# Linear attention and a Fourier mix: key pieces, masks and conversions of the first batch in other places of a fixed order, folded sums on one engine, and the last group's pieces paced otherwise

## Chip, cores and metric

The kernel runs on one core of a Trainium2 chip. The metric is the device time of one execution in microseconds, as the median of several runs. A profiled execution gives a trace besides: what each engine did and when. The engines are PE (TensorE: matmuls and transposes), DVE (VectorE), ACT (ScalarE), POOL (GpSimd) and SP, which here only issues transfers.

## The reference

Two parts follow each other. The first is a "delta rule" linear attention for B = 4 batches, H = 8 heads, S = 768 tokens, D = 48. Every head carries a 48x48 state through the tokens, one after the other:

```python
k_n = k / (np.linalg.norm(k, axis=-1, keepdims=True) + 1e-06)
for t in range(S):
    y[:, :, t] = np.einsum('bhd,bhde->bhe', q[:, :, t], state)
    v_old = np.einsum('bhde,bhd->bhe', state, kt)
    state = state + bt[:, :, :, None] * np.einsum('bhd,bhe->bhde', kt, vt - v_old)
```

The heads are then laid side by side (768 tokens x 384 channels per batch), and the second part is a Fourier mix with an MLP:

```python
mixed = np.real(np.fft.fft(np.fft.fft(x, axis=1), axis=2))
u = x + mixed
un = (u - mean(u)) / np.sqrt(var(u) + 1e-06)
return u + np.maximum(un @ w_ch1, 0.0) @ w_ch2
```

w_ch1 is 384x1536 and w_ch2 1536x384; both come as float64 and all else is float32.

## The kernel before

**Attention.** Tokens are cut into chunks of 64, so a batch has 12 chunks and the whole work 48 chain steps m. A step (`chain`, L671-728) has three parts: pc products of keys and state, with U = V − pc on DVE; products with the inverted triangular matrix wt, copied by ACT; and the state's sum `st` on DVE. Each part waits for the one before, so the chain is a string of short hand-overs between PE, DVE and ACT. After every second step two chunks' outputs `y` are computed (`outputs`, L732-769: products py, then an ACT copy and a DVE sum into x).

Four chunks form a quad Q, two quads a group g (eight steps). What a group's steps need is made ahead in *pieces*: `prepare` (L413-484; `keys` and `queries` are halves of it) transposes keys and queries (pt on PE, KQT on ACT), makes their grams (pg on PE, A on ACT), and for the queries a masked gram LQ. In the first quads the mask is a multiply of its own on DVE, `masks(Q)` (L405-411, two instructions a quad). `invert(g)` (L500-572) inverts the triangular matrices by 30 pairs of DVE operations (A, then X), and `Merge`/`merge` (L574-648) joins blocks to larger ones (pj on PE, wt on ACT). `values` and `loads` issue the transfers of v, k and q on SP, most of them at L219.

**Fourier and MLP.** `fourier(b)` (L798-920) starts when a batch's outputs are complete. `folded` (L816-828) adds and subtracts the token halves (into scr, or hT for batch 0), then folds the channels: the sum F<-scr at L826 and a small copy of two edge columns at L828. `shifted` (L830-841) builds six combinations of the three tiles. Then come matmuls pf, ACT copies to F, matmuls pb, DVE sums into x, and the layernorm's statistics. `mlps` (L924-991) is one generator over all batches: normalise (un), transpose (ptr, unT), 12 blocks of ph with a ReLU on ACT, and po products that DVE adds to x; then the store.

**Weights.** A float64 weight is turned into float32 in three moves (L300-315): `digits`, two ACT operations; `joined`, two DVE operations and one add on POOL. The first weight is twelve pieces (`FirstWeight`, L317-356): `fetch` starts the transfer, `split(p)` runs the digits, `join` yields after each of its 36 operations, and fetches pieces 10 and 11 on SP into the stages of pieces 0 and 1. `second_weight` (L358-386) does the same with three stages that lie in x tiles of later batches.

**What sets the order.** Through the first batch the order on PE, DVE and ACT is written out by hand (`strict`, L123-137; it holds each instruction behind the one before in the program; POOL and DMA are free). The loop at L1086-1122 goes over steps m = 1 to 11 and, after each of the three parts i, emits other work: `key_work` (L1083) gives how many of the twelve key pieces of quads 4 and 5 (eight pt with their copies, four pg) come after part i of step m; `rest` (L1084) is a sequence of the 36 join operations and the 2 masks of quad 3; `masks(1)`, `masks(2)`, `w.split(10)` and `w.split(11)` have fixed steps; at steps 10 and 11 the first `fourier(0)` begins. From step 12 on (L1131-1212) a scheduler orders the instructions by their dependencies and by the order of emission, and the loop paces that emission: each part of a step adds to `due[0]` (how many pieces of the next group to emit) and to `due[1]` (how many pieces of Fourier and MLP work). The constants are

```python
PRE, SIDE = 2.4, (0.0, 1.3, 2.0, 1.8)
```

and 4.6 takes the place of PRE in group 1. A group's last pieces, where they aren't out yet, are run at the step that needs them. A group's pieces begin at m % 8 = 1; group 5, the last, is prepared from m = 33 on and used from m = 40. After step 47 the Fourier work of batch 3 and the rest of the MLP end the program (L1208-1212).

Of the kernel before, what the change touches and what calls it, by code (L numbers as in the profile page):

```python
# [82 lines left out]
def kernel(  # L83
# [11 lines left out]
    B, H, S, D = q.shape  # L95
    DM = H * D
# [7 lines left out]
    TH = NC // 2  # L104
    HD = DM // 2
# [31 lines left out]
    dve, act, pe = Ordered(nc.vector), Ordered(nc.scalar), Ordered(nc.tensor)  # L137
    pool = nc.gpsimd
# [158 lines left out]
    def words(stage):  # L297
        return stage[:, :, 0], stage[:, :, 1]

    def digits(stage, low, mag):  # L300

        lo, hi = words(stage)
        act.activation(low, lo.bitcast(mybir.dt.uint32), ACT.Copy, scale=2.0 ** -29)
        act.activation(mag.bitcast(F32), hi.bitcast(F32), ACT.Copy, scale=2.0 ** -112)
# [50 lines left out]
    def second_weight():  # L358
        if moe_w_ch1.dtype == F32:
            yield  # L360
            nc.sync.dma_start(out=w2, in_=moe_w_ch2.rearrange("(c p) m -> p c m", p=128))
            converted.update(range(KF))
            return
        w2v = moe_w_ch2.bitcast(I32).rearrange("(c p) (m two) -> p c m two", p=128, two=2)

        stages = [xpairs[i].rearrange("p t (f two) -> p (t f) two", two=2).bitcast(I32) for i in (4, 5, 6)]

        def fetched(p):
            if p < KF:
                nc.sync.dma_start(out=stages[p % 3], in_=w2v[:, p])  # L370

        for p in range(3):
            fetched(p)
        yield
        digits(stages[0], *words(stages[0]))
        for p in range(KF):
            if p + 1 < KF:
                digits(stages[(p + 1) % 3], *words(stages[(p + 1) % 3]))
            ops = joined(w2[:, p], *words(stages[p % 3]))
            ops[0]()  # L380
            yield
            ops[1]()
            ops[2]()
            fetched(p + 3)
            converted.add(p)
            yield
# [411 lines left out]
    def fourier(b):  # L798
# [14 lines left out]
        def widths(a):  # L813
            return (HD + 1, 1) if a == 0 else (HD - 1, 0)

        def folded(a, Ts, helped):  # L816

            op = ALU.add if a == 0 else ALU.subtract
            w, o = widths(a)
            eo = zs[a][:, 0:TH * DM].rearrange("p (t d) -> p t d", t=TH)  # L820
            ed = eds[a][:, 0:TH * w].rearrange("p (t d) -> p t d", t=TH)
            for T in Ts:
                dve.tensor_tensor(eo[:, T], x[T][:, 0], x[T][:, 1], op=op)
            ts = slice(min(Ts), max(Ts) + 1)
            eng = pool if helped else dve
            eng.tensor_tensor(ed[:, ts, o:o + HD - 1], eo[:, ts, 1:HD], eo[:, ts, DM - 1:HD:-1], op=op)  # L826
            if a == 0:
                (pool if b < B - 1 else dve).tensor_copy(ed[:, ts, 0:HD + 1:HD], eo[:, ts, 0:HD + 1:HD])  # L828

        def shifted(a):  # L830

# [11 lines left out]
        if b == 0:  # L843
            for T in range(TH - 1, -1, -1):
                mixed_sums = []
                for a in range(2):
                    folded(a, [T], False)
                    if T == 0:
                        mixed_sums.append(shifted(a))
                        yield  # L850
                if T > 0:
                    yield
        for a in range(2):
            w = widths(a)[0]
            if b > 0:
                folded(a, range(TH), a == 0 and b < B - 1)
            if b > 0:
                z = shifted(a)
                yield
            else:  # L860
                z = mixed_sums[a]
            n6 = 65 if a == 0 else 64
            for i in range(2):
                rows = min(128, w - 128 * i)
                dc = slice(128 * i, 128 * i + rows)
                pf = ps_one([128, 512], "pf")
                pr = pf[0:rows, 0:384].rearrange("p (r k) -> p r k", k=64)
                c0 = 0 if a == 0 else 641

                parts = [(0, n6, pf[0:rows, 320:320 + n6]), (1, 64, pr[:, 2]),  # L870
                         (2, 128, pr[:, 0:5:4]), (3, 128, pr[:, 0:5:4]),
                         (4, 128, pr[:, 1:4:2]), (5, 128, pr[:, 1:4:2])]
                for zi, n, dst in parts:
                    mm(dst, z[:, zi, dc], stab[:, c0:c0 + n], zi == 0)
                    c0 += n
                act.activation(F[0:rows, a, i].rearrange("p (k r) -> p r k", r=6), pr, ACT.Copy)
                if a == 0:
                    act.activation(gz[0:rows, i, 31:32], pf[0:rows, 384:385], ACT.Copy)
                yield
# [4 lines left out]
        for T in tiles(b):  # L884
            pb = ps_one([128, DM], "pb")
            ts = slice(128 * T, 128 * T + 128)
# [109 lines left out]
    def advance(gen, n=1):  # L996
        for _ in range(n):
            if next(gen, "end") == "end":
                return False
        return True  # L1000

    def run(*gens):
        for gen in gens:
            for _ in gen:
                pass
# [67 lines left out]
    T = lambda l, step: lambda: merges[l].taken(step)  # L1073
# [6 lines left out]
                (8, 1): T(3, 0), (9, 1): Dg(3), (10, 1): T(3, 1)}  # L1080

    next_keys = keys(4, 5)
    key_work = {(7, 0): 2, (8, 2): 3, (9, 0): 1, (10, 2): 2, (11, 0): 1, (11, 1): 2, (11, 2): 1}  # L1083
    rest = seq(w.join(), masks(3))  # L1084
    first_mixing = fourier(0)
    for m in range(1, NCH):  # L1086
        if m == 3:
            merges.update({2: Merge(1, 0, crossed=False), 3: Merge(1, 1, crossed=False)})
        for i, _ in enumerate(chain(m)):
            if pe_work[m][i]:  # L1090
                pe_work[m][i]()
            if m == 2 and i > 0:
                outs()
            if (m, i) in act_work:
                act_work[m, i]()
            advance(next_keys, key_work.get((m, i), 0))
            if i == 1:
                if m == 1:
                    run(masks(0))
                    advance(first)  # L1100
                elif m == 2:
                    scaled(1)
                    advance(first)
                elif m == 3:
                    run(masks(1))
                elif m == 6:
                    scaled(2)
                    advance(rest, 2)
                elif m == 8:
                    run(masks(2))  # L1110
                    advance(rest, 1)
                elif m == NCH - 1:
                    scaled(3)
                    advance(rest, 3)
                else:
                    advance(rest, 5)
            if i == 2:
                advance(rest, 1)
                if m in (3, 7):
                    w.split(10 + m // 7)  # L1120
                if m in (10, 11):
                    advance(first_mixing)
    run(rest, *later)
    later.clear()
    advance(first_mixing)
    second = second_weight()
    advance(second)

# [38 lines left out]
    PRE, SIDE = 2.4, (0.0, 1.3, 2.0, 1.8)  # L1167
    pre, due, started = ahead(2), [0.0, 0.0], False
    for m in range(NCH, STEPS):
        b, n = divmod(m, NCH)  # L1170
        g, Q = m // (2 * QT), m // QT

        count = 0
        while Q not in merged:
            advance(pre)
            count += 1
            if len(converted) == KF and (m <= 2 * NCH or count % 2 == 0):
                beside()
        if m % (2 * QT) == 1:
            run(pre)  # L1180
            pre = ahead(g + 1) if g + 1 < NG else iter(())
            due = [0.0, 0.0]
        for i, _ in enumerate(chain(m)):
            if i < 2:
                advancing(later)
            if n == 0 and i == 1:
                run(*later)
                later.clear()
                if b == 1:
                    while advance(first_mixing):  # L1190
                        if (0, 0) in norms or started:
                            started = advance(channels, 2)
                else:
                    mixing[0] = fourier(b - 1)
                    fresh.append(b)
            if b == 1 and (n > 0 or i > 1):
                advance(second, 3)
            if m > NCH or i > 0:
                due[0] += 4.6 if g == 1 else PRE
                due[1] += SIDE[b]  # L1200
            while max(due) >= 1.0:
                if due[1] >= 1.0:
                    due[1] -= 1.0
                    beside()
                if due[0] >= 1.0:
                    due[0] -= 1.0
                    advance(pre)
# [35 lines left out]
```

## Time and profile before

| | |
|---|---|
| runs | 764.0, 764.2, 766.97, 766.98 us; median 765.58 |
| profiled execution | 763.36 us, its span 761.6 us |
| mean granted PE clock | 0.98 |
| PE busy | 677.9 us, 89% of the span, 7806 matmuls |
| DVE busy | 391.4 us, 51%, 987 instructions |
| ACT busy | 260.9 us, 34%, 708 instructions |
| POOL busy | 80.3 us, 11%, 114 instructions |
| largest groups | ph 864 matmuls, 207.3 us; po 600, 203.8 us |
| DMA | 30.78 MB, mean 40 GB/s |

Busy time is a sum over the whole span. In the page's slices, 40 of equal length (19 us each), a digit is the busy share in tenths, and PEclk the TensorE clock that was granted. A group's row gives the line and engine, what is written and read, the count, and then busy time, mean time of one and idle time before it with what released it. L131 is the helper through which nearly all instructions of PE, DVE and ACT go, so these are told apart by tile names. The chain of waits is followed back from the last instruction, each piece of time given to the work that released what came after. In the timeline, the bracket holds the idle time before an instruction and its releaser.

### The profile page before, as it was taken

To read this page: it belongs to the slowest core of one execution; us is meant where nothing else is said; L and a number is where in the kernel's file an instruction comes from. 1 tells how busy PE (TensorE), PEld (TensorE's weight loads), DVE (VectorE), ACT (ScalarE), POOL (GpSimd) and SP (SyncE) were. 2 spreads that over 40 slices of the span, in tenths; PEclk is the share of its full clock that TensorE was granted. 3 is DMA by queue.
4 is the path that set the end of the run, shared out by engine and by line. 5 is a ranking of instruction groups with operands and counts; after the bars stand their busy time and mean duration, and the time that the engine had idled before them with its cause. 6 is when DMAs were issued, how large, how long until landed. Compare 5 with 4: busy or idle time off the path is not lost.

```text
span 761.6 us, 18377 instructions
## 1 busy us (share of the span) xinstructions
PE 677.9 (89%) x7806; PEld 492.1 (65%) x7806; DVE 391.4 (51%) x987; ACT 260.9 (34%) x708; POOL 80.3 (11%) x114
## 2 busy tenths in 40 slices
PE   5935498888989989989998999878999999899998
PEld 4623487666757657576756667456658677577686
DVE  2599776788980289546498121787711114600000
ACT  3742354743325522444413445111532122021120
POOL 8010024223100010010000000011000000200000
PEclk9999999989999999979999999988999999999999
DMA  8643033342220230112101110100100000000000
GB/s 181 170 106 55 6 85 62 87 131 70 40 41 18 38 68 14 31 24 42 28 22 25 25 36 10 22 22 1 23 12 11 12 12 1 21 1 22 10 11 21
DMA packets 81185, 30.78 MB, mean 40 GB/s; under 512 B 75872, under 2 KB 77536, under 8 KB 81104
## 3 DMA queue, kind: packets, MB, share of 16 engines
q1 hardware_dynamic: 76704, 21.92, 14.1%
q0 software_dynamic: 2224, 7.31, 3.1%
q8 instruction: 61, 1.00, 0.5%
q10 hardware_dynamic: 2176, 0.39, 0.3%
q14 instruction: 20, 0.16, 0.1%
HBM read 24.87 MB, written 4.72 MB: 39 GB/s over the span
## 4 chain that ended last, share of the span: by engine, by line
PE 57%; DVE 25%; ACT 5%; SPq 5%; DMA 4%; issue 3%; POOL 1%; ACTq 0%; DVEq 0%; POOLq 0%
PE po L131 19%; PE ph L131 18%; DVE A L131 5%; PE pc L131 5%; DVE X L131 5%; PE pf L131 3%; DVE x L131 3%; SPq L219 3%; DVE w L131 3%; PE pj L131 3%; PE pt L131 2%; DMA qp<-in_q_dram 2%; PE py L131 2%; PE pg L131 2%; ACT A L131 2%
## 5 line engine op out<-in xcount | busy, mean ns | idle before, releaser
L131 PE MATMUL ph<-unT,w 128*128 128x256 f32 x864 | 207.3, 390 | 4.9 <-ACT hT L131 2.9
L131 PE MATMUL po<-w,hT 128*128 128x384 f32 (+1 forms) x600 | 203.8, 485 | 0.3 <-ACT unT L131 0.3
L131 PEld LDWEIGHTS ph<-unT,w 128*128 128x128 f32 x864 | 159.3, 191 | 32.9 <-ACT hT L131 5.8
L131 PEld LDWEIGHTS po<-w,hT 128*128 128x128 f32 x600 | 107.7, 190 | 60.1 <-issue 1.7
L131 ACT ACTIVATE hT<-ph 128x256 f32<-128x256 f32 x144 | 54.9, 382 | 183.2 <-PE ph L131 182.8
L131 DVE TENSOR_TENSOR x<-x,po 128x384 f32<-128x384 f32 (+1 forms) x25 | 13.4, 535 | 99.2 <-PE po L131 99.2
L131 DVE TENSOR_TENSOR U<-V,pc 128x192 f32<-128x192 f32 x48 | 16.8, 350 | 72.9 <-PE pc L131 72.8
L131 PE MATMUL pg<-KQT 48*64 48x64 f32 (+1 forms) x1152 | 45.0, 295 | 5.9 <-ACT KQT L131 4.5
L131 PEld LDWEIGHTS pg<-KQT 48*64 48x64 f32 x1152 | 34.2, 176 | 21.5 <-ACT KQT L131 11.0
L787 POOL DMA_INDIRECT out_dram<-x,rows_hi x12 | 12.4, 1031 | 327.1 <-DVE x L131 183.2
L131 ACT ACTIVATE KQT<-pt 128x256 f32<-128x256 f32 (+1 forms) x84 | 33.2, 414 | 30.5 <-PE pt L131 29.6
L131 DVE TENSOR_TENSOR A<-X 128x30 f32<-128x30 f32 (+14 forms) x120 | 40.8, 340 | 3.0
L131 DVE TENSOR_TENSOR X<-X,A 128x30 f32<-128x30 f32 (+14 forms) x120 | 40.5, 338 | 3.0
L131 ACT ACTIVATE U<-pc 128x192 f32<-128x192 f32 x48 | 15.9, 332 | 70.5 <-PE pc L131 67.3
L131 DVE TENSOR_TENSOR st<-st,pc 128x192 f32<-128x192 f32 x44 | 15.4, 350 | 39.7 <-PE pc L131 29.6
L131 PE MATMUL pt<-pack,qp 128*128 128x128 f32 x96 | 22.6, 331 | 13.7 <-DMA qp<-in_q_dram 12.7
L131 PEld LDWEIGHTS pc<-st,KQT 48*64 48x64 f32 x768 | 19.5, 156 | 22.2 <-DVE st L131 9.6
L131 PE MATMUL pc<-st,KQT 48*64 48x48 f32 x768 | 26.4, 251 | 6.9 <-DVE st L131 6.3
L131 PEld LDWEIGHTS pc<-U,wt 64*64 64x64 f32 x768 | 19.4, 155 | 20.0 <-issue 8.7
L131 DVE TENSOR_TENSOR x<-x,pb 128x191 f32<-128x191 f32 (+1 forms) x72 | 24.9, 411 | 14.5 <-PE pb L131 14.5
L131 ACT ACTIVATE wt<-pj 32x128 f32<-32x128 f32 (+1 forms) x84 | 23.7, 283 | 23.0 <-PE pj L131 22.2
L131 ACT ACTIVATE A<-pg 128x256 f32<-128x256 f32 (+1 forms) x72 | 25.3, 378 | 16.2 <-PE pg L131 15.6
(140 smaller groups left out, 849.7 us busy)
## 6 DMA issues: line engine op xcount, KB each, us to landing
x<-in_moe_w_ch_dram SPq DMA_DIRECT2D x14, 384.0 KB, 4.3
qp<-in_q_dram SPq DMA_DIRECT2D x96, 48.0 KB, 2.7
kp<-in_k_dram SPq DMA_DIRECT2D x80, 48.0 KB, 2.9
V<-in_v_dram SPq DMA_DIRECT2D x56, 48.0 KB, 2.7
w<-in_moe_w_ch_dram POOLq DMA_DIRECT2D x6, 384.0 KB, 8.1
x<-in_moe_w_ch_dram POOLq DMA_DIRECT2D x4, 384.0 KB, 7.6
V<-in_v_dram SPq DMA_DIRECT2D x64, 24.0 KB, 2.2
out_dram<-x SPq DMA_DIRECT2D x7, 192.0 KB, 1.9
```

The source lines that it names most:

```text
L131: ins = getattr(self.engine, name)(*args, **kwargs)
L219: eng.dma_start(out=vals[Q][64 * p:64 * p + CH, cs, u, :], in_=v[b, 4 * (p ^ (u % 2)) + u, t0:t0 + w * CH, :].rearrange("(c p) d -> p c d" ...
L787: nc.gpsimd.indirect_dma_start(out=out.rearrange("b s m -> (b s) m"), out_offset=bass.IndirectOffsetOnAxis(ap=rows_hi[:, i:i + 1], axis=0) ...
```

## The change

There are five edits. Key pieces: their numbers at the steps are changed, nine of twelve come in the loop, and the last three after the first fold of batch 0's Fourier work. `masks(1)` goes from step 3 to step 4, and `split(10)` from step 3 to step 5. The pieces of `rest` get other counts per step. `folded` uses DVE throughout, where the sum of L826 was on POOL for the first half of batches 1 and 2, and the copies of L828 on POOL for batches 0 to 2. And in the last batch (b = 3, m from 36) `due[0]` grows by nothing in its first two steps and by 3.2 a part from then on, where it grew by 2.4.

```diff
-        def folded(a, Ts, helped):
+        def folded(a, Ts):
...
-            eng = pool if helped else dve
-            eng.tensor_tensor(ed[:, ts, o:o + HD - 1], eo[:, ts, 1:HD], eo[:, ts, DM - 1:HD:-1], op=op)
+            dve.tensor_tensor(ed[:, ts, o:o + HD - 1], eo[:, ts, 1:HD], eo[:, ts, DM - 1:HD:-1], op=op)
             if a == 0:
-                (pool if b < B - 1 else dve).tensor_copy(ed[:, ts, 0:HD + 1:HD], eo[:, ts, 0:HD + 1:HD])
+                dve.tensor_copy(ed[:, ts, 0:HD + 1:HD], eo[:, ts, 0:HD + 1:HD])
...
-    key_work = {(7, 0): 2, (8, 2): 3, (9, 0): 1, (10, 2): 2, (11, 0): 1, (11, 1): 2, (11, 2): 1}
+    key_work = {(7, 2): 2, (8, 2): 1, (9, 2): 2, (10, 2): 2, (11, 1): 2}
...
-                elif m == 3:
+                elif m == 4:
                     run(masks(1))
                 elif m == 6:
                     scaled(2)
-                    advance(rest, 2)
                 elif m == 8:
                     run(masks(2))
-                    advance(rest, 1)
                 elif m == NCH - 1:
                     scaled(3)
-                    advance(rest, 3)
-                else:
-                    advance(rest, 5)
+                advance(rest, {4: 1, 5: 2, 6: 3, 7: 5, 8: 1, 9: 2, 10: 5, 11: 3}.get(m, 0))
             if i == 2:
-                advance(rest, 1)
-                if m in (3, 7):
+                advance(rest, 2 if m > 3 else 1)
+                if m in (5, 7):
                     w.split(10 + m // 7)
                 if m in (10, 11):
                     advance(first_mixing)
     run(rest, *later)
     later.clear()
     advance(first_mixing)
+    run(next_keys)
...
-                due[0] += 4.6 if g == 1 else PRE
+                due[0] += 4.6 if g == 1 else PRE if b < B - 1 else 3.2 if n > 1 else 0.0
```

## What was predicted

> **What bounds the kernel now.** I read the page's busy times and slices first, then the busy times by stretch, then the chain of waits at each place the diff touches, then the timeline there. TensorE (PE) is busy in 677.9 of 761.6 us, but not evenly:
>
> ```profile
> PE   5935498888989989989998999878999999899998
> DVE  2599776788980289546498121787711114600000
> PEclk9999999989999999979999999988999999999999
> ```
>
> The stretches say where PE's idle time lies (columns: stretch, length, PE, PEld, DVE, ACT, POOL busy, granted clock, DMA share, GB/s):
>
> ```profile
> 80.00:240.00 160.00, 140.04 (x2121) 109.09 (x2122) 118.76 (x288) 71.88 (x194) 33.55 (x43) 0.98 0.27 64
> 240.00:480.00 240.00, 228.36 (x2943) 162.04 (x2943) 125.65 (x333) 96.73 (x279) 12.09 (x14) 0.98 0.15 29
> 480.00:540.00 60.00, 49.90 (x487) 35.29 (x486) 49.03 (x142) 9.63 (x22) 6.96 (x10) 0.89 0.07 15
> 540.00:640.00 100.00, 98.77 (x1147) 69.05 (x1146) 26.08 (x61) 30.79 (x89) 2.04 (x2) 1.00 0.04 12
> 640.00:761.60 121.60, 116.33 (x486) 86.00 (x484) 17.95 (x49) 18.32 (x44) 6.88 (x10) 1.00 0.04 14
> ```
>
> PE idles 20.0 us in 80 to 240 us, 11.6 in 240 to 480, 10.1 in 480 to 540, 1.2 in 540 to 640 and 5.3 in the rest. After about 172 us the filler (the MLP's matmuls) keeps PE at work nearly throughout, and its sum isn't changed. So the change is worth what it does to PE's idle time and to stretches at half clock. Up to 172 us PE waits for the 12 chain steps of the first batch; there the chain of waits rules (start, length, what):
>
> ```profile
> 105.91 1.29 DVE LQ L131 x2
> 107.20 0.28 DVE st L131
> ...
> 122.00 1.04 PE pt L131 x4
> ...
> 131.09 3.08 DMA x<-in_moe_w_ch_dram
> ...
> 142.72 1.04 PE pt L131 x4
> ...
> 146.56 0.88 PE pg L131 x32
> ```
>
> Four things stand between one step and the next: a mask (LQ), key pieces (pt, pg) and an ACT that waits for a transfer.
>
> [...] The trace has the folded sum on both, 1400 against 753 ns, 1.86 times[...].
>
> ```profile
> L131 DVE TENSOR_TENSOR F<-scr 128x573 f32<-128x573 f32 x4 | 3.0, 753 | 0.1
> L826 POOL TENSOR_TENSOR F<-scr 128x573 f32<-128x573 f32 x2 | 2.8, 1400 | 17.1 <-DVE scr L131 17.1
> ```
>
> [...] the inversion's 0.38 us multiply takes 1.43 beside the folded sum on POOL:
>
> ```profile
> 496.16 1.40 POOL L826 TENSOR_TENSOR F<-scr 128x573 f32<-128x573 f32 x1 [13.17 <-DVE scr L131]
> 496.37 1.43 DVE L131 TENSOR_TENSOR X<-X,A 128x220 f32<-128x220 f32 x1
> ```
>
> [...] The trace grants 0.50 from about 495.3 to 502.1 us, after PE had nothing from 493.1 on. [...] the sum x<-x,py, ready at about 489.6, ran at 494.67, behind an operation that waited 2.76 us for a V transfer.
>
> **The change part by part** (earlier is negative). I walked the order of instructions of both programs on each engine, with durations from the rows of before.
>
> *Masks(1) at step 4.* The two LQ (1.29) stood between step 3's U and its state sum. There the step now ends with the wt projections (pj), so it starts step 4 only 0.9 earlier. At step 4 they lie beside pj of 1.04 and ACT's copies.
>
> *Join pieces.* Before step 6 stand four join operations on DVE (0.48 to 0.74 each), two of them now: −1.3. The 36 joins and 2 masks stay; they go to steps whose DVE has room (7 and 10). Joining issues two of the weight's fetches on SP, in the same steps as before, so SP's queue isn't changed by it; split(10) at step 5 lies after its transfer.
>
> *Key pieces.* They issue no DMA: a piece is four small transposes (pt, 1.04 per four or 0.44 per two) or a gram (pg, 0.88 to 1.1), and its ACT copies. At step 7 pt stays ahead of the next step's first product (nothing). At step 8 one pt group goes: −1.0. At step 9 pg (1.1) leaves, and ACT's A copies no longer stand behind the 3.08 us of transfer: −1.6, between 0 and −3 since that transfer may be late elsewhere. Step 10 takes over a piece: +0.9. Step 11 loses pg and two pt: −1.4. The last three pieces run behind the first fold, whose VectorE operations no longer have a 1.04 us transpose (X<-A) ahead of them, and whose F copy is a DVE operation (0.2) and not a trip to POOL (0.45 with two hand-overs): −1.2.
>
> The chain so reaches the first Fourier matmul (pf at 158.36) by 0.9 + 1.3 + 1.0 + 1.6 − 0.9 + 1.4 + 1.2 = 6.5 us earlier at most; the pieces put behind it take back some 1.7 (pg 0.88, two pt groups 0.44 each): 4.8. Two things may eat it. ACT's conversion of the second weight waits for a fetch behind 16 V transfers on SP (0.74 us each, 11.8), so F<-pf comes only 3 earlier, x<-pb 3.9. But V4's multiply (0.96 and a 1.2 wait for its DMA) falls behind the second group's inversion, which so ends 4.7 earlier. I take −4.6 for the head, bounds −7 and −1.5: −7 if the hidden waits vanish too; −1.5 if the V transfers set the end[...].
>
> *Folded sums on VectorE.* Fourier of batch 1 (328 us): on the path POOL 1.40 + 0.20 and two hand-overs of about 0.1 become DVE 0.75 + 0.17: −0.9, bounds 0 (DVE's queue is full there) and −1.5. Fourier of batch 2 (496 us): the same, but in DVE's strict queue an inversion multiply, a copy of another sum and an A row come before it, +0.2; nothing gained by this part alone. The DVE time added is 2 × 0.92; DVE is busy 51%.
>
> *Pieces of the last group two steps later.* No work is added; order moves. At the 2-to-3 boundary two more po groups fill PE and the inversion stands one or two rows further back when pb and un come: −1.1, bounds 0 and −4. The 2.76 us wait for V stays.
>
> In the tail the cost comes back. The filler of batch 2 that now runs earlier, while no pieces are pushed, isn't there later. After the chain's last py (about 628.9) nine ph groups (4.08 us) and 24 po (15.5) cover Fourier of batch 3 before, 20 po (12.9) after: 4.08 + 15.5 − 12.9 = 6.7 us of cover less. The road from py to the first ph of batch 3 has 33.9 us before, with about 2 of idle:
>
> ```profile
> 660.62 0.49 PE L131 MATMUL ptr<-pack,un 128*128 128x128 f32 x3
> 661.69 0.55 PE L131 MATMUL ptr<-pack,un 128*128 128x128 f32 x3 [0.58 <-DVE mv L131]
> 662.81 1.56 PE L131 MATMUL ph<-unT,w 128*128 128x256 f32 x6 [0.58 <-ACT unT L131]
> ```
>
> With less cover it takes about 27.9 (the pf, pb, VectorE chain is then the bound): 6.0 shorter for 6.7 less work, and I put idle at 4.8 and not 2: +2.7. Three of its waits (3.0, 1.25 and 0.55) then lie within 6 us[...], so +1.0 on average. Tail +3.7, bounds +1 and +8.
>
> Sum: −4.6 − 0.9 + 0 − 1.1 + 3.7 = −2.9. The profiled execution took 763.36 us (span 761.6 and 1.8 around it), 2.2 below the runs' median 765.58; so the same profile would show about 760.5, and the median moves to 765.58 − 2.9 = 762.7.
>
> **The rivals.**
> 1. *The tail keeps its cover.* For: before, 3 us of idle there left the clock at 1.00. Then the head gives −5.0, the boundaries −2.0, the tail +0.5: −6.5, 759.1.
> 2. *Slower: the tail starves.* One mechanism: the 6.7 us of filler gone ahead leave PE idle one for one (the road is not shortened, because DVE's rows bound it), and the gaps take PE to half clock[...] (10 us, +5.0): +11.7, against −6.6 at most elsewhere: +5.1, 770.7. It decides from a tail loss of 6.6 us on. Against: the road holds 13 us of po matmuls in front of pb, which must lie somewhere.
> 3. *Little happens.* The gain of the first batch is lost again at the V transfers (before the second inversion both sides wait for the same 11.8 us on SP), −1.5, boundaries −0.5, tail +1.7: 765.3.
>
> **How the numbers follow.** Likeliest (head's gain partly given back in the tail) 0.50, 762.7, its own range 759.5 to 766. Rival 1 0.31, rival 2 0.12, rival 3 0.07. A difference of 0.5% (3.8 us) is about what a measurement of this kernel can tell from no change. Faster than 761.8: 0.15 of the first case, 0.26 of rival 1: 0.41. Slower than 769.4: most of rival 2, 0.10, and 0.01 of the first: 0.11. The rest 0.48. The range reaches from head and boundaries at their better bounds (−7 − 2) to near rival 2: 756.5 to 769.5; 0.08 lies below, 0.11 above.
>
> **What would show it.** PE idle in 80 to 240 us falls from 20.0 to about 15.5, pf starts near 153.6, no LQ and no 3.08 us transfer in the chain before step 10. POOL has no L826 row; two more DVE F<-scr of about 750 ns. PE idle after the last py is near 5 us, and the clock there tells between likeliest and rival 2. I am wrong if pf doesn't start 3 us earlier, if the V fetches hold the second group's inversion, or if the tail's PE idle exceeds 8 us.

## The result and the profile after

The changed kernel took 769.49 us (median of 34 executions, 762.26 to 777.39), the kernel before, beside it, 764.75 (55 executions, 760.37 to 767.95). The ratio to the kernel before is 1.0035, 95% interval 1.0018 to 1.0052: slower, by less than the 0.5% that I had called the limit of this measurement; the medians differ by 4.7 us, 0.6%. The ratios here and below leave out executions more than 1.5% above the fastest of their kernel (eight of the changed kernel's, of 774 us and more, three each of runs 2 and 6, two of run 5, one of run 3), the medians and means don't. The profiled execution took 770.76 us, span 769.0. The prediction was 762.7, faster; the sign was wrong, and 769.49 lies at the very edge of its range.

The page's busy times and slices of the kernel after:

```profile
PE 689.5 (90%) x7806; PEld 498.4 (65%) x7806; DVE 395.2 (51%) x994; ACT 260.9 (34%) x708; POOL 77.1 (10%) x107
...
PE   5934599979999989989999999798999999799998
DVE  2599777987980289446597113887511114600000
...
PEclk9999999998999999979999999989999999799999
```

PE does the same 7806 matmuls and is busy for 11.6 us longer (689.5 against 677.9), while it idles 4.2 us less (769.0 − 689.5 = 79.5 against 83.7). So the change did take idle time out. About half of the longer busy time is matmuls that ran slower: 41.4 us at half clock against 30.8 in the two traces, worth 5.3. The other half isn't more work either, but I have not broken it down. Records of matmuls overlap (in the timelines sixteen of pc take 0.45 us together, one alone 0.25), so busy time can also grow where small ones stand apart. The last row has a 7 in its 35th slice, near 660 us, where before there is a 9. The busy times by stretch, kernel after (stretch, length, PE, PEld, DVE, ACT, POOL busy, granted clock, DMA share, GB/s):

```profile
80.00:240.00 160.00, 144.54 (x2118) 110.24 (x2119) 121.66 (x292) 72.05 (x194) 33.96 (x40) 0.98 0.27 64
240.00:480.00 240.00, 228.76 (x2936) 162.50 (x2936) 124.77 (x328) 95.87 (x277) 10.39 (x12) 0.97 0.15 29
480.00:540.00 60.00, 52.23 (x511) 37.40 (x504) 49.30 (x150) 10.49 (x25) 5.19 (x8) 0.91 0.08 16
540.00:640.00 100.00, 98.99 (x1135) 68.48 (x1134) 23.56 (x52) 28.97 (x85) 2.03 (x2) 1.00 0.04 12
640.00:769.00 129.00, 120.56 (x498) 89.14 (x496) 21.99 (x59) 20.04 (x48) 6.75 (x10) 0.96 0.04 13
```

Idle in 80 to 240 us is 15.5, from 20.0, the number foretold. It is not time gained by 240 us: nearly the same matmuls (2118 and 2121) count as busy for 4.5 us longer, and chain step 16 comes at the same time in both (below). In the last stretch it is 8.4, from 5.3, and the clock there is 0.96 and not 1.00.

**Where the lag arises.** I followed both kernels by their landmarks: the time of the kernel after minus that of before.

| landmark | before | after | lag |
|---|---|---|---|
| chain step 4, first product | 107.51 | 106.66 | −0.9 |
| step 9 | 132.21 | 129.08 | −3.1 |
| step 11 | 143.69 | 139.99 | −3.7 |
| first pf of batch 0 | 158.36 | 154.74 | −3.6 |
| first pb of batch 0 | 167.11 | 162.52 | −4.6 |
| first ph of batch 0 | 177.07 | 175.34 | −1.7 |
| step 16 | 238.48 | 238.50 | 0.0 |
| first pf of batch 1 | 331.32 | 331.51 | +0.2 |
| step 28 | 383.17 | 385.42 | +2.3 |
| first ptr of batch 2 | 519.61 | 520.17 | +0.6 |
| first ptr of batch 3 | 660.61 | 661.20 | +0.6 |
| ptr after that | 678.45 | 685.81 | +7.4 |

The head's gain is there (−4.6) and is gone at step 16. The tail, between the last two rows, loses 6.8 us. The order of the work in between differs, so rows there are less exact: the third tile's pb stands ahead of the first ptr of batch 3 before (1.66 us) and behind it after. And each column is one execution. Run 1 below is the same program as the kernel before up to step 36, yet its trace is 4.3 us late there; a lag of a few us in one trace is not by itself the work of an edit. PE's timeline in the tail of the kernel after, and the stretches around it:

```profile
656.46 1.77 PE L131 MATMUL pb<-dtab,F 128*128 128x193 f32 x8
661.25 0.55 PE L131 MATMUL ptr<-pack,un 128*128 128x128 f32 x3 [3.02 <-DVE un L131]
662.38 0.59 PE L131 MATMUL ptr<-pack,un 128*128 128x128 f32 x3 [0.58 <-ACT unT L131]
663.54 2.93 PE L131 MATMUL ph<-unT,w 128*128 128x256 f32 x6 [0.58 <-ACT unT L131]
```

```profile
650.00:660.00 10.00, 8.23 (x32) 4.99 (x32) 5.99 (x17) 0.85 (x1) 1.21 (x3) 1.00 0.06 20
660.00:670.00 10.00, 7.59 (x22) 5.59 (x23) 4.58 (x15) 1.36 (x3) 1.62 (x3) 0.64 0.00 0
670.00:680.00 10.00, 9.53 (x39) 7.72 (x38) 2.58 (x9) 2.30 (x6) 0.93 (x2) 0.85 0.01 2
```

The first wait is the 3.0 us that the prediction computed. What follows is a clock of 0.50 from 662.8 to 673.0 us: six matmuls ph take 2.93 us, where the same took 1.56 before. In the head the stretch of half clock, 157.4 to 164.2 us before, lies at 171.2 to 178.1 after. Two stretches there, first before, then after:

```profile
160.00:170.00 10.00, 9.78 (x128) 8.54 (x129) 7.21 (x21) 6.44 (x15) 2.80 (x3) 0.79 0.58 179
170.00:180.00 10.00, 8.71 (x106) 5.86 (x99) 8.77 (x29) 4.66 (x11) 3.39 (x4) 1.00 0.39 111
```

```profile
160.00:170.00 10.00, 7.43 (x100) 5.24 (x99) 8.23 (x24) 6.13 (x14) 3.43 (x5) 1.00 0.48 129
170.00:180.00 10.00, 9.88 (x58) 7.12 (x59) 6.58 (x23) 2.32 (x6) 2.87 (x4) 0.66 0.29 85
```

**A measure for the clock.** In the traces of both kernels the clock is 1.00 or 0.50 and nothing between. If that holds in every execution, its mean granted clock c gives its time at half clock, 2 × (1 − c) × span: 41.5 us for the profiled execution after, whose single stretches add up to 41.4 inside the span (the last one reaches beyond its end). Over all executions of a kernel it has a mean, and time less half of it is about what the kernel would take at full clock (a little too low, since a stretch in which PE waits costs less: the 6.8 us in the head of the kernel before cost about one, by its steps below). Over 36 executions of the kernel after the time follows its clock closely (correlation −0.96). All runs (executions with a profile are counted in, so 36 and not 34; for the kernel before beside the changed kernel the record has times and no clocks):

| kernel | executions | median us | ratio to before (95%) | mean time at half clock | rest at full clock |
|---|---|---|---|---|---|
| before, beside runs 1 to 4 | 54 | 764.99 | 1 | 33.1 | 748.5 |
| before, beside runs 5 to 8 | 43 | 763.46 | 1 | 31.6 | 747.5 |
| before, beside runs 9 to 11 | 19 | 764.56 | 1 | 31.6 | 748.6 |
| changed | 36 | 769.49 | 1.0035 (1.0018 to 1.0052) | 41.8 | 748.4 |
| 1 pacing alone | 6 | 771.17 | 1.0085 (1.0061 to 1.0109) | 45.4 | 749.0 |
| 2 changed, old pacing | 22 | 763.71 | 0.9955 (0.9931 to 0.9980) | 31.5 | 746.6 |
| 3 order alone | 17 | 763.99 | 0.9972 (0.9949 to 0.9994) | 36.2 | 745.2 |
| 4 folds alone | 22 | 762.28 | 0.9963 (0.9950 to 0.9977) | 30.1 | 746.9 |
| 5 changed, matmuls in the gap | 22 | 763.54 | 0.9980 (0.9958 to 1.0002) | 29.6 | 747.8 |
| 6 changed, filler held back | 22 | 758.96 | 0.9939 (0.9916 to 0.9963) | 31.4 | 743.7 |
| 7 run 2 and matmuls in the head | 6 | 756.47 | 0.9904 (0.9876 to 0.9931) | 20.1 | 746.1 |
| 8 runs 6 and 7, new pacing | 6 | 753.02 | 0.9870 (0.9844 to 0.9897) | 16.3 | 744.9 |
| 9 before, matmuls in the head | 14 | 764.08 | 0.9996 (0.9980 to 1.0011) | 29.8 | 749.1 |
| 10 run 8 with the old pacing | 6 | 756.91 | 0.9907 (0.9876 to 0.9937) | 22.7 | 745.7 |
| 11 run 8 and more matmuls | 6 | 757.95 | 0.9920 (0.9895 to 0.9944) | 22.9 | 746.5 |

The changed kernel has 8.7 us more of half clock than the kernel before beside runs 1 to 4, worth some 4.4, and nothing else worth a microsecond.

### The profile page after: what moved, and what is told of

The parts are those of the page before. It is cut to its first block, busy times and chain, and to the rows that moved or that the text cites. A ratio compares the mean times of both kernels' runs of the same rounds, so it can differ in the third digit from the quotient of the medians.

```text
span 769.0 us, 18377 instructions
## 1 busy us (share of the span) xinstructions
PE 689.5 (90%) x7806; PEld 498.4 (65%) x7806; DVE 395.2 (51%) x994; ACT 260.9 (34%) x708; POOL 77.1 (10%) x107
## 4 chain that ended last, share of the span: by engine, by line
PE 59%; DVE 24%; ACT 6%; SPq 3%; issue 3%; DMA 3%; POOL 0%; ACTq 0%; DVEq 0%
PE ph L131 19%; PE po L131 18%; DVE A L131 6%; PE pc L131 5%; DVE X L131 5%; PE pg L131 3%; SPq L219 3%; DVE w L131 3%; PE pj L131 3%; PE pf L131 3%; PE pt L131 2%; DVE x L131 2%; PE pb L131 2%; PE py L131 2%; ACT A L131 1%
## 5 line engine op out<-in xcount | busy, mean ns | idle before, releaser
L131 PE MATMUL ph<-unT,w 128*128 128x256 f32 x864 | 213.4, 397 | 5.7 <-ACT hT L131 3.2
L131 PEld LDWEIGHTS ph<-unT,w 128*128 128x128 f32 x864 | 162.2, 195 | 35.8 <-ACT hT L131 6.6
L131 PEld LDWEIGHTS pg<-KQT 48*64 48x64 f32 x1152 | 34.9, 178 | 22.6 <-ACT KQT L131 10.9
L131 DVE TENSOR_TENSOR A<-X 128x30 f32<-128x30 f32 (+14 forms) x120 | 41.5, 345 | 3.1
L131 PE MATMUL pt<-pack,qp 128*128 128x128 f32 x96 | 22.7, 333 | 12.6 <-DMA qp<-in_q_dram 12.0
L131 ACT ACTIVATE A<-pj 32x128 f32<-32x128 f32 (+1 forms) x76 | 20.7, 273 | 35.1 <-PE pj L131 34.3
```

The costliest lines, as they stand in the source:

```text
L131: ins = getattr(self.engine, name)(*args, **kwargs)
```

## The experiments

Theory A, formed on these traces: the new pacing takes filler from the tail, the gap brings half clock, and the head's gain is spent at half clock too. Its rivals are B, the folds or the new order cost; C, no edit costs, and the executions spread widely; later D, the idle time itself costs and not the clock; E, the pacing costs in the chain; F, the head's gain is lost to a wait for data; G, the added matmuls help anywhere; H, the new pacing is worth nothing.

**1. The pacing alone.** The kernel before, with one line of the change:

```diff
-                due[0] += 4.6 if g == 1 else PRE
+                due[0] += 4.6 if g == 1 else PRE if b < B - 1 else 3.2 if n > 1 else 0.0
```

> The kernel before with one edit, the pacing of the last group's pieces (nothing in two steps, then 3.2 a part). Theory A (the pacing takes filler out of the tail; PE idles there and then runs at half clock): +6 us against the kernel before, between +3 and +9, with PE idle before the tail's first transposes of un of about 3 us and a granted clock of 0.50 for 7 to 10 us from about 660 us on. Theory B (the loss comes from the folded sums or the new order of the first batch; pacing is harmless): within 1.5 us of before, clock 1.00 in the tail. Theory C (no single edit costs[...]): within 2 us on the median, with a spread over 8 us between executions.

Ratio 1.0085, 6.5 us: theory A, and B falls. PE's timeline of this run, tail, and one stretch:

```profile
665.13 0.90 PE L131 MATMUL ptr<-pack,un 128*128 128x128 f32 x3 [3.03 <-DVE un L131]
666.61 0.90 PE L131 MATMUL ptr<-pack,un 128*128 128x128 f32 x3 [0.58 <-ACT unT L131]
668.10 2.93 PE L131 MATMUL ph<-unT,w 128*128 128x256 f32 x6 [0.58 <-ACT unT L131]
```

```profile
660.00:670.00 10.00, 5.80 (x22) 3.83 (x21) 7.53 (x23) 0.98 (x2) 2.82 (x5) 0.68 0.06 20
670.00:680.00 10.00, 9.53 (x30) 7.09 (x29) 3.21 (x10) 1.15 (x3) 0.92 (x2) 0.64 0.00 0
```

The same gap of 3.0 us, and half clock from 663.5 to 677.2, 13.7 us, more than the 7 to 10 expected. In the table the edit adds 12.3 us at half clock (6.2 of time) and 0.5 us otherwise.

**2. All but the pacing.** The changed kernel with that line undone.

> The changed kernel with the old pacing. Theory A: the loss in the tail is gone; the new order and folds remain: 762 to 765 us, 0 to 3 us under the kernel before, clock 1.00 from 640 us on. Theory B: as slow as the changed kernel, about 769. Theory C: as spread as the changed kernel, median 766 to 769.

Ratio 0.9955, 3.4 us faster than before (1.3 by the medians): order and folds are a gain, and the pacing turns it over. With run 1's +6.5 that makes +3.1, and the changed kernel's ratio stands for +2.7. The trace has clock 1.00 from 640 to 755 us. Theory A on the median; the spread between executions (754.9 to 769.45) is C's, so a part of C stands: the same program meets more or less half clock from one execution to the next (granted clock 0.968 to 0.989).

**3. The order of the first batch alone.** `key_work`, masks(1), the joins, split(10) and the last three pieces as in the change, folds and pacing as before.

> The kernel before with the new order of the first batch alone (key pieces, masks, joins, split). Theory A: step 12 and the first Fourier matmul some 2.5 to 3.5 us earlier (the copies of the fold stay on POOL and take about 1 of the changed kernel's 3.6), of which half or more is lost at half clock by 240 us: -0.5 to -2 us in the end. Theory B (if the order is the culprit): +3 to +5 us. Theory C: within 1 us on the median.

Ratio 0.9972, −2.1 us, a little more than A's range and inside the interval. In its profiled execution the first pf stands at 153.8, 4.5 us earlier, and half clock comes at 159.7 to 166.6 and again at 173.4 to 183.6: at step 16 it is 2.6 us later than before. The copies on POOL cost nothing visible here.

**4. The folds alone.**

> The kernel before with all folded sums on VectorE and nothing else. Theory A: first Fourier matmul of the first batch about 1 us earlier, at 328 us 0 to 1 earlier, at 496 us nothing: 0 to -1.5 us in the end. Theory B (if the folds are the culprit, because VectorE's queue is full at the batch boundaries): +2 to +5 us, with the inversion beside it later. Theory C: within 1 us.

Ratio 0.9963, −2.8 us, nearly twice A's best. The first pf is 1.1 us earlier, as expected. At the boundary of batches 2 and 3, on DVE's timeline, the multiply that stood beside POOL, 1.43 us before, is short again, 0.38:

```profile
495.76 0.74 DVE L131 TENSOR_TENSOR F<-scr 128x573 f32<-128x573 f32 x1
496.42 0.38 DVE L131 TENSOR_TENSOR X<-X,A 128x220 f32<-128x220 f32 x1
496.72 0.15 DVE L131 COPY F<-scr 128x6 f32<-128x6 f32 x1
497.14 0.62 DVE L131 TENSOR_TENSOR scr<-F 128x193 f32<-128x193 f32 x2
498.09 2.36 PEld L131 LDWEIGHTS pf<-stab,scr 128*128 128x128 f32 x12 [2.62 <-DVE scr L131]
```

(In the kernel after, the list of groups has six sums F<-scr of 752 ns on DVE and none on POOL.) From scr<-x to the first pf it is 3.27 us, before 3.40, so the path there gains 0.1; at batch 1 it is 3.22 for 3.38, 0.2. Half of the gain is clock: 3.0 us less at half clock, 1.5 of time; the other 1.6 are in the rest.

So the folds' own path doesn't give 2.8 us. What is much shorter in this trace is the road from step 36 to batch 2's first ptr, 30.8 us for 34.9, and what differs there is a transfer that DVE waits for, first before, then in this run:

```profile
491.91 0.96 DVE L131 TENSOR_TENSOR V<-V,ln 128x768 f32<-128x768 f32 x1 [2.76 <-DMA V<-in_v_dram]
491.30 0.96 DVE L131 TENSOR_TENSOR V<-V,ln 128x768 f32<-128x768 f32 x1 [0.43 <-DMA V<-in_v_dram]
```

The wait doesn't follow the folds: it is 0.62 in run 3, which has the old ones, and 2.19 in the changed kernel. Over all traces it is 2.2 to 2.8 us in four (before, changed, runs 1 and 9), each with 6.8 us of half clock next to it, and 0.65 or less in the other nine, with 3.4 or none. Why the transfer is late in some is not shown, and so neither is where the folds' 2.8 us come from.

**5. Is it the gap or the clock?** The changed kernel, with three matmuls that nothing reads, in the gap of the tail:

```diff
+    def warm(lhsT, n):
+        o = ps_pair("idle", "ch")[:, 0, 0:384]
+        for _ in range(n):
+            mm(o, lhsT, stab[:, 0:384], True)
...
+                if b == B - 1:
+                    warm(x[T][:, 1, 0:128], 3)
```

> The changed kernel with three matmuls of no use put on PE in the tail, into a PSUM tile that nothing reads, where PE stands idle for 3.0 us between the product pb of the second tile and the transposes of un. They neither bring filler back nor shorten a wait. Theory A (the tail's loss is mostly PE at half clock after the idle gap): clock 1.00 from 640 us on in most executions, 3 to 5 us faster than the changed kernel, 764 to 767 us. Theory D (the loss is the idle time itself, the starvation; the clock is only its sign): no faster than the changed kernel, 769 to 771 us, since the same gaps stay and three matmuls are added.

763.54 us, a little under A's 764; ratio 0.998 to the kernel before, where the changed kernel has 1.0035 and the intervals don't overlap. By the ratios that is 4.2 us, inside A's 3 to 5. Tail of the run's trace (a float32 matmul stands there as two records, so the three make x6):

```profile
659.88 2.20 PE L131 MATMUL idle<-stab,x 128*128 128x384 f32 x6
662.00 0.59 PE L131 MATMUL pb<-dtab,F 63*128 63x191 f32 x2
663.04 0.55 PE L131 MATMUL ptr<-pack,un 128*128 128x128 f32 x3 [0.45 <-DVE un L131]
664.17 0.55 PE L131 MATMUL ptr<-pack,un 128*128 128x128 f32 x3 [0.58 <-ACT unT L131]
665.30 1.56 PE L131 MATMUL ph<-unT,w 128*128 128x256 f32 x6 [0.58 <-ACT unT L131]
```

```profile
660.00:670.00 10.00, 8.24 (x35) 5.30 (x34) 7.64 (x23) 1.48 (x4) 1.88 (x4) 1.00 0.05 20
```

From pd to the transposes it takes 5.0 us, against 5.6 in the changed kernel: no wait has become shorter by the amount saved. The six ph are back at 1.56. Mean time at half clock falls from 41.8 to 29.6 us. (The traced execution shows the tail and not the mean: it took 768.26 us and has as much half clock as the changed kernel's, but elsewhere, 27 us of it between 159 and 218 us.) So theory D falls: work of no use in a gap makes the kernel faster, and the larger part of the tail's loss is the clock.

**6. Bring the filler back.** The changed kernel with less filler spent beside the last batch's chain:

```diff
-    PRE, SIDE = 2.4, (0.0, 1.3, 2.0, 1.8)
+    PRE, SIDE = 2.4, (0.0, 1.3, 2.0, 1.6)
```

> The changed kernel with the filler of the last batch paced at 1.6 instead of 1.8 pieces a part: after the chain's last outputs 15 ph groups and 24 po are left in the order of PE, where the changed kernel has 0 and 20 and the kernel before 9 and 24. Pacing of the last group's pieces stays as in the changed kernel. Theory A (missing filler is what makes the gap and so the half clock): tail idle back to 2 us or less, clock 1.00 from 640 us on, 760 to 764 us. Theory E (the pieces' pacing itself costs, in the chain of the last batch): still 767 to 770 us.

758.96 us, better than A's range. The stretch that holds the same road shows it; the gap of 3.0 us is 0.3 here:

```profile
650.00:660.00 10.00, 9.10 (x36) 6.13 (x36) 4.52 (x13) 1.50 (x4) 2.33 (x4) 1.00 0.05 20
```

Here idle time falls too (the rest at full clock is 4.7 below the changed kernel's, of which about one is also in the kernel before beside it, on that chip). The missing filler made the gap, and theory E falls.

**7. The head.** Run 2 with two more such matmuls near 168 us, where PE waits for ACT's copy of U:

```diff
                 for t in range(2):
-                    unread(x[T][:, t, 0:128])
+                    for _ in range((2, 2)[t]):
+                        unread(x[T][:, t, 0:128])
```

> The changed kernel with the old pacing (as in the second run of this study), and in the first batch's Fourier work four matmuls of no use instead of two, where PE waits near 168 us for ACT. Theory A (the head's gain of about 4 us is lost because a half-clock stretch now falls at 171 us, where PE has work): no stretch of 0.50 between 165 and 180 us in most executions, mean time at half clock 5 us or more below that of the run without it, 760 to 762 us. Theory F (the head's gain is lost to a wait for data, such as the V transfers or the second weight's fetches): no faster than without, 763 to 765 us.

756.47 us: 4 us under A's 760, the ratio falls from 0.9955 to 0.9904. The stretch 170 to 180 us, first of run 2, then of this run:

```profile
170.00:180.00 10.00, 10.00 (x54) 7.33 (x55) 7.80 (x26) 2.47 (x6) 3.23 (x5) 0.66 0.31 90
```

```profile
170.00:180.00 10.00, 9.45 (x80) 7.11 (x79) 8.18 (x27) 4.34 (x10) 3.59 (x5) 1.00 0.31 90
```

54 matmuls in ten full microseconds at 0.66, 80 at 1.00. The half clock from 171.8 to 178.6 us of run 2's trace is gone; one execution of each is traced, so "in most executions" isn't shown. Mean time at half clock falls by 11.4 us, the rest hardly (746.6 and 746.1). So theory F falls as the whole account. But the gap ahead of the half clock is a wait for data. In the changed kernel ACT's copy of U stands behind a conversion that waits for the second weight's transfer (in run 2 for 1.73 us; in run 8 for 1.97, but with the four matmuls and no half clock behind it):

```profile
168.88 0.98 ACT L131 ACTIVATE x<-x 128x384 int32<-128x384 uint32 x2 [2.15 <-DMA x<-in_moe_w_ch_dram]
169.76 0.31 ACT L131 ACTIVATE U<-pc 128x192 f32<-128x192 f32 x1
```

In the kernel before this copy comes at 169.32, ahead of such a wait.

**8. Both.** The changed kernel with the edits of runs 6 and 7.

> The changed kernel with both: filler paced at 1.6, and the four matmuls near 168 us. Theory A: the sum of the two, 758 to 762 us, faster than both kernels. Theories E and F: no better than 763 us.

753.02 us, 5 under A's range, 0.9870 (0.9844 to 0.9897): faster than either kernel. In its profiled execution two stretches of half clock are left before the end, near 325 and 513 us.

**9. The head's matmuls in the kernel before.**

> The kernel before with four matmuls of no use instead of two in the first batch's Fourier work. Theory A (what counts is whether a half-clock stretch falls where PE has work): little to win, 0 to -2 us, since before the head's stretch of half clock lies at 157 to 164 us, ahead of these matmuls and while PE waits for the chain anyway. Theory G (these matmuls help by themselves, in any order of the first batch, by some 6 us): 757 to 759 us.

0.9996: nothing. So these matmuls are no gain by themselves (theory G falls). They pay where the first batch's new order has moved PE's idle time to 168 us, in front of work that PE could be doing.

**10. The old pacing, with cover and head repaired.**

> As the run with both (filler paced at 1.6, four matmuls near 168 us), but with the old pacing of the last group's pieces. Theory A with the prediction's sum for the boundary of batches 2 and 3 (the new pacing saves 1.1 us of idle there, 0 to 4): 1 to 3 us slower than with the new pacing, 754 to 756 us. Theory H (the new pacing is worth nothing where the tail is covered): as fast as with it, 752 to 754 us.

756.91 us, ratio 0.9907 against 0.9870. The rest at full clock, each less that of the kernel before beside it, is −2.9 here and −2.6 with the new pacing; the difference is the clock (22.7 and 16.3 us). It points the way of A, but the intervals meet and there are six executions of each: whether the new pacing is worth anything, with the tail covered, stays open. Against run 7 this run differs in the filler alone, and the ratios are the same (0.9904 and 0.9907): less filler beside the chain shows no gain by itself there, so what it brought in run 6 is most likely what the new pacing had taken from the tail.

**11. More of the same.** Single matmuls after the first tile of batches 1 and 2 as well.

> As the run with both, and one matmul of no use twice in the Fourier work of batches 1 and 2 too, after the sums of their first tile. Theory A: mean time at half clock, 16 us in the run with both, falls by 3 us or more, and the time by 1 to 2 us, 751 to 752 us. If those stretches fall while PE waits anyway, or the matmuls push others back: no gain, 753 to 755 us.

757.95 us, outside both ranges: by the ratios 3.8 us slower than run 8 (the intervals just meet, six executions each) and with more half clock (22.9 us). In its profiled execution the stretch near 328 us is still there, 10.2 us long. Putting such matmuls anywhere doesn't do it; they also take their place in PE's order.

## Why the prediction was wrong, by its steps

- **Masks, joins, key pieces.** Right, nearly to the tenth up to step 11: the sum of the steps up to step 9 was −0.9 − 1.3 − 1.0 = −3.2, measured −3.1; with −1.6 at step 9 −4.8, measured −4.7 at step 10; with +0.9 −3.9, measured −3.7 at step 11; at the first pf I had −4.8 and found −3.6, at the sums behind pb −3.9, where pb itself shows −4.6. One us of that is the clock: from the first pf to the first pb it takes 8.75 us before, most of it at half clock, and 7.78 after. So the −4.6 that I took for the head came out there in part by luck. The chain after has no LQ and no transfer before step 10. Its 3.08 us of transfer has become 4.1 us further on:

```profile
134.74 0.65 PE pc L131 x16
...
152.56 4.09 DMA x<-in_moe_w_ch_dram
...
157.18 0.55 ACT x L131
```

- **−4.6 at pb as −4.6 at the end.** This step failed. My −4.6 had no half clock in it. The stretch of half clock before lay at 157 to 164 us and cost about the one us above, since the chain set the pace there. The new order has PE's idle time at 168 to 170 us, and 6.8 us of half clock fall on full work from 171 us on, worth 3.4; runs 2 and 7 show that the clock matters there. The rest of the loss goes with the wait ahead of it: the conversion of the second weight, which I had named as one of two things that might eat the gain, holds ACT's copy of U, and PE idles 1.93 us for it. Nor is it the order in every execution: run 1's trace, with the old head, has half clock from 175.4 to 182.2 us. Over many executions not all is lost, −2.1 us in run 3.
- **Folds.** −1.2 and −0.9 and nothing at 496 us make −2.1; run 4 has −2.8. That is near by luck: the first pf came 1.1 earlier, but at batch 1 the path gained 0.2 for 0.9 (the sums behind the fold start 0.7 earlier, but on DVE the fold now stands ahead of U, whose products PE has ahead of pf), and the shorter road in run 4's trace is at the boundary of batches 2 and 3, where I had nothing.
- **Pacing, boundary of batches 2 and 3, −1.1.** From step 36 to batch 2's first ptr the lag goes from +1.9 to +0.6, −1.3, with 6.8 us of half clock in both: the number, but not the pacing's work. Run 1, with the pacing alone, gains only 0.2 there (4.3 before the boundary, 4.1 at the first pb behind it), and run 2, with the new folds and the old pacing, 5.4. No run shows the gain, and run 10 leaves it open.
- **Pacing, tail, +3.7.** Here the sum broke; this is the step that turned the sign. The gap was right, 3.02 us for 3.0, and the idle time, 8.4 − 5.3 = 3.1 for 2.7. The term for half clock, +1.0 on average, was an estimate of mine that no trace stood behind, and it was mis-sized. Half clock measured 10.2 us in the changed kernel's profile and 12.3 us on average in run 1: 5 to 6 us of time. With this one term at its measured size the sum is +1 to +2. Set against the runs: for the pacing I had −1.1 + 3.7 = +2.6, and run 1 has +6.5; for order and folds −4.6 − 0.9 = −5.5, and run 2 has −3.4.
- **Rivals.** Rival 2's mechanism came: a starved tail with some 10 us of half clock. That its 770.7 is near is luck: it had +11.7 for the tail and −6.6 elsewhere, and both were too large (6.8 between the last two landmarks, with 3.1 of idle and not 6.7; −3.4 in run 2). The rival with a covered tail came nearest in run 6, where I covered it: −4.5 us by the medians for its −6.5.

In the traces of both kernels the stretches of half clock are 3.41, 6.83 or 10.24 us long, but for the last of each, which reaches beyond the end of the program; run 1's in the tail has 13.7. I had treated half clock behind the gap as a matter of chance, and that was a guess. Both traces with the gap of 3.0 us and the waits of 0.6 behind it have it: over the 3.41 us before the clock fell PE was 27% busy in the changed kernel and 58% in run 1. Whether it comes in every execution isn't shown.

## What to carry to other kernels

Where PE is the bound and runs near full, take every piece of work moved ahead of a wait as a piece of cover taken from that wait, and price the gap that opens with its clock: here 3 us of gap were followed by 10 to 14 us at half rate. Idle time moved from a place where PE waits for others to one with work behind it need not be a gain, even if the chain is shorter (here −4.6 us at the first pb and 0.0 at step 16); look at where each half-clock stretch lies before and after, not at the mean. Compare kernels over many executions and by their granted clock.

## What the runs showed of the hardware

The time of one program on one core spread over 15 us (762.26 to 777.39), and nearly all of that goes with the granted clock (0.984 to 0.960, correlation −0.96). Half clock didn't come behind idle time alone: in the changed kernel's trace, taken in pieces of 3.41 us that line up with its stretches of half clock, PE was 27% busy in the piece before the tail's stretch and 43% in the one before the head's; pieces of 52% (from 413.6 us) and 59% (from 382.9) were not followed by half clock, while two of 65% (from 324.8) and 68% (from 352.1) were. So the busy time of one such piece doesn't decide it, and what does isn't shown. And matmuls that nothing reads made the kernel faster, in run 5 three of them (763.54 us, the changed kernel 769.49), in run 7 two (756.47, run 2 763.71), but not in run 9 (0.9996).
